# The last matrix of a decode step: w4 rows in four array columns, smaller last pieces, and a result stored in two parts

## The chip, the cores and the metric

The kernel runs on one core of a Trainium2 chip. A core has five engines that matter here: TensorE (PE in the profile; PEld is its loading of weights), VectorE (DVE), ScalarE (ACT), GpSimd (POOL) and SyncE (SP), which issues DMAs. Sixteen DMA engines move data between the chip's memory (HBM) and the core's on-chip memory (SBUF, 128 partitions). TensorE writes into eight accumulating banks (PSUM), from which VectorE and ScalarE read. The metric is the device time of one execution in microseconds, lower being better; three runs of the kernel before gave a median of 400.46 us.

## The reference

One token of a decode step, width D = 1024, all in bf16. The input is normalized, then goes through an attention block and an MLP-like block, and all are added:

```python
xn = _layernorm(x)
return x + A(xn) + B(xn)

# A: 32 query heads, 4 key/value heads, 65536 cached keys of 128
q = xn @ wq
o = softmax(q @ k.T * 128**-0.5) @ v
A = o @ wo                                  # wo: 4096 x 1024

# B: one token, so the shifts of the mixer leave zeros
h = gelu(layernorm(xn) @ w1)
x1 = xn + shifted(h) @ w2                   # shifted(h) is zero for one token
B = x1 + gelu(layernorm(x1) @ w3) @ w4      # w3: 1024 x 3584, w4: 3584 x 1024
```

So what is left after the attention is a row vector of 1024: the attention's result times wo, plus the activated row of 3584 times w4, plus two copies of normalized or plain x.

## The kernel before

Everything streams. SP issues all loads of the large arrays in one order (`stream`, line 285): wq, w3, w1 and w2, then eight pairs of K and V blocks of 8 MB each, then wo (8 MB) and w4 (7 MB). Three SBUF slots of 128 x 32768 bf16 take them in turn, so a load waits until the matmuls on what lay in its slot three loads earlier are done (`freed`, line 311). There is no scheduler: a small recorder (`Program`, line 49) takes each engine's instructions in the order in which the code names them, and `plan` (line 124) adds a semaphore wait only where a read or a write meets an earlier one of another engine or of a DMA.

For each K block, VectorE transposes it in 32x32 blocks and TensorE multiplies it with the queries into the bank tensor `sc` (four banks, `scores`, line 456); VectorE finds the maxima, ScalarE takes the exponentials, and TensorE multiplies with the V block into `oacc` (`values`, line 490). After a pair of blocks, `group_rows` (line 509) adds up a group of heads into `oT`, the attention's result laid out for a matmul.

What follows is the end of the kernel, and the place of the change. wo is 32 and w4 is 28 "rows": in row c, each partition holds 1024 numbers, and a column of 128 numbers (`oT[:, c]` or `hT[:, c]`) multiplies them. The stationary operand is that column repeated 32 times, so a matmul uses an array column of 32 out of 128 and leaves 32 equal rows in PSUM. `row_acc` (line 342) uses two array columns, j = 0 and 1, each for 512 of the 1024 result columns, and adds into the bank `psB`. Its first use is the w2 product (line 438), then wo (line 544), then the w4 rows up to the last `NARROW` = 8 (line 548).

The last eight w4 rows run in `narrow_rows` (line 554), in four array columns: q = 2h + j takes 256 result columns, h = 0 into the bank pm0 and h = 1 into pm1. After `AHEAD` = 5 of them, VectorE's sum of psB and the x part (`sums`, line 552) is added into pm0 and pm1 by two small matmuls with the selector `pick` (line 564), and the last three rows follow.

w4 comes in five loads, `W4_PIECES` = 8, 12, 5, 2 and 1 rows (line 299), all issued together as soon as the last K block is free. The pieces' matmuls wait for them one after the other. At the end ScalarE copies pm0's 256 columns to bf16 and VectorE pm1's, both into `x_halves` (lines 569 and 570), and ScalarE's queue issues one store of partitions 31 and 32, which hold the two halves of the result (line 571). Then ScalarE clears the semaphores and SP waits for the store to land (line 581).

Of the kernel before, what the change touches and what calls it, by code (L numbers as in the profile page):

```python
# [14 lines left out]
P = 128  # L15
ROW = 32768
SUBS = 4
SETS = 4
W4_PIECES = (8, 12, 5, 2, 1)
NARROW = 8  # L20
AHEAD = 5

WIDTH = {F32: 4, BF16: 2}

# [182 lines left out]
def kernel(  # L207
# [14 lines left out]
    nc = tc.nc  # L222
    D = A_x.shape[-1]
# [7 lines left out]
    FC = F // P  # L231
    UKEYS = P * ROW // DH
    assert DH == P and HQ // HKV == 8 and HKV == 4 and D == 1024 and F == 3584 and S == 1
    assert SK == 2 * UKEYS and sum(W4_PIECES) == FC
    NB = 2
# [3 lines left out]
    COLS = (P, 32)  # L239

    prog = Program(nc)
    pe, dve, act, pool = prog, prog.dve, prog.act, prog.pool

    def sb(name, shape, dtype=F32):
        return nc.alloc_sbuf_tensor(name, list(shape), dtype)

    def ps(name, shape):
        return nc.alloc_psum_tensor(name, list(shape), F32)
# [4 lines left out]
    x_row = sb("x_row", [32, D], BF16)  # L253
# [4 lines left out]
    x_halves = sb("x_halves", [64, 512], BF16)  # L258
    qdiag = sb("qdiag", [P, LEAD + 4 * P], BF16)
    g_col = sb("g_col", [P, 1], BF16)  # L260
# [9 lines left out]
    hT = sb("hT", [P, FC], BF16)  # L270
    oT = sb("oT", [P, 32], BF16)
    ol = sb("ol", [P, DH + 1])
    pick = sb("pick", [64, 2, 32])

    sc = ps("sc", [P, SUBS, 512])
    oacc = ps("oacc", [P, 512])
    pm = [ps(f"pm{i}", [P, 512]) for i in range(2)]
# [8 lines left out]
    tiles = {it: slots[i % 3] for i, it in enumerate(stream)}  # L286

    def load(it):
        t = tiles[it]
        if it == "wq":  # L290
            prog.load("sp", t[:], A_wq.rearrange("(p c) n -> p (c n)", c=DC))
        elif it == "w3":
            prog.load("sp", t[:, 0:DC * F], B_w3.rearrange("(p c) f -> p (c f)", c=DC))
        elif it == "w12":
            prog.load("sp", t[:, 0:DC * D], B_w1.rearrange("(p c) n -> p (c n)", c=DC))
            prog.load("sp", t[:, DC * D:2 * DC * D], B_w2.rearrange("(m c) n -> m (c n)", c=DC))
        elif it == "wo":
            prog.load("sp", t[:], A_wo.rearrange("(p j) n -> p (j n)", p=P))
        elif it == "w4":
            w4_v = B_w4.rearrange("(m c) n -> m c n", c=FC)  # L300
            c0 = 0
            for n in W4_PIECES:
                prog.load("sp", t[:, c0 * D:(c0 + n) * D], w4_v[:, c0:c0 + n, :].rearrange("p c n -> p (c n)"))
                c0 += n
        else:
            kind, i = it
            g, b = divmod(i, NB)
            cache = A_k_cache if kind == "K" else A_v_cache
            prog.load("sp", t[:], cache[0, g, b * UKEYS:(b + 1) * UKEYS, :].rearrange("(p ct) d -> p (ct d)", p=P))

    def freed(it):

        n = stream.index(it) + 3
        if n < len(stream):
            load(stream[n])

    load("wq")
    opening = len(prog.ops)

    dve.memset(x_row[:], 0.0)  # L320
    prog.load("act", x_row[0:1, :], A_x[0, 0:1, :])
    load("w3")
    load("w12")

# [9 lines left out]
    for b in range(2):  # L334
        pool.tensor_copy(
            out=spread[:, 2 * b:2 * b + 2, :].rearrange("p r (a i) -> p r a i", a=4),
            in_=ident_f[:, 64 * b:64 * b + 64].rearrange("p (i r) -> p r i", r=2).unsqueeze(2).to_broadcast([P, 2, 4, 32]))
    pool.memset(x_halves[:], 0.0)
    pool.memset(qdiag[:], 0.0)
    pool.memset(g_col[:], 0.0)  # L340

    def row_acc(j, lhsT, rhs, start=False):
        return pe.mm(psB[32 * j:32 * j + 32, :], lhsT.to_broadcast([P, 32]), rhs, start, False, (0, 32 * j), COLS)

    x_t = p_sb[:, 0:DC * 32].rearrange("p (c j) -> p c j", j=32)
    for a in range(4):
        dve.transpose(out=x_t[32 * a:32 * a + 32].rearrange("p c j -> p (c j)"),
                      in_=x_row[:, 256 * a:256 * (a + 1)].rearrange("p (i c) -> p c i", c=DC))
    dve.tensor_copy(out=xT[:], in_=x_t[:, :, 0])

    def layernorm(src, tag):
# [24 lines left out]
    _, xn2_rep, _, _ = layernorm(xn, "b")  # L376
# [6 lines left out]
                    in_=sel8[:].unsqueeze(1).unsqueeze(3).to_broadcast([P, 4, 8, 4]))  # L383
    dve.tensor_copy(out=pick[:],
                    in_=ident_f[0:64, 0:64].rearrange("p (j r) -> p j r", r=32)[:, :, 0:1].to_broadcast([64, 2, 32]))
    dve.tensor_scalar(out=ln_s1[:], in0=rstd1[:], scalar1=1.0, scalar2=None, op0=ALU.add)
    dve.tensor_tensor(out=ln_s2[:], in0=negmean1[:], in1=rstd1[:], op=ALU.mult)
    for j in range(2):
        dve.tensor_copy(out=x_halves[32 * j:32 * j + 1, :], in_=x_row[0:1, 512 * j:512 * (j + 1)])

    def row_matmul(rep, cols, widths):
        for c in range(DC):
# [37 lines left out]
    def compute_w12():  # L430
        wt = tiles["w12"][:, 0:2 * DC * D].rearrange("p (w c n) -> p w c n", w=2, c=DC)
        for c in range(DC):
            for q in range(2):
                pe.mm(sc[0:32, q, :], xn2_rep[:, c, :], wt[:, 0, c, 512 * q:512 * (q + 1)], c == 0, c == DC - 1,
                      (0, 0), COLS)
        h1 = p_sb[0:32, 0:1024].rearrange("p (q n) -> p q n", q=2)
        act.activation(out=h1, in_=sc[0:32, 0:2, :], func=ACTF.Gelu_apprx_tanh)
        for c in range(DC):
            for j in range(2):
                row_acc(j, g_col[:], wt[:, 1, c, 512 * j:512 * (j + 1)], start=(c == 0))  # L440
        freed("w12")

    W = ROW // SETS
# [80 lines left out]
    compute_wq()  # L524
    compute_w3()
    compute_w12()
    for u in range(NU):
        g, b = divmod(u, NB)
# [11 lines left out]
    o = tiles["w4"][0:64, FC * D:FC * D + D].bitcast(F32)  # L540
    dve.tensor_scalar(out=o, in0=x_halves[:], scalar1=ln_s1[0:64, 0:1], scalar2=ln_s2[0:64, 0:1],
                      op0=ALU.mult, op1=ALU.add)

    for j in range(32):
        for h in range(2):
            row_acc(h, oT[:, j:j + 1], tiles["wo"][:, D * j + 512 * h:D * j + 512 * (h + 1)])
    wt = tiles["w4"]
    for c in range(FC - NARROW):
        for j in range(2):
            row_acc(j, hT[:, c:c + 1], wt[:, D * c + 512 * j:D * c + 512 * (j + 1)])  # L550
    sums = og[0:64, :]
    dve.tensor_tensor(out=sums, in0=psB[0:64, :], in1=o, op=ALU.add)

    def narrow_rows(lo, hi, start=False):
        for c in range(lo, hi):
            for h in range(2):
                for j in range(2):
                    q = 2 * h + j
                    pe.mm(pm[h][32 * q:32 * q + 32, 0:256], hT[:, c:c + 1].to_broadcast([P, 32]),
                          wt[:, D * c + 512 * j + 256 * h:D * c + 512 * j + 256 * (h + 1)], start and c == lo, False,  # L560
                          (0, 32 * q), COLS)

    narrow_rows(FC - NARROW, FC - NARROW + AHEAD, start=True)
    for h in range(2):
        pe.mm32(pm[h][64 * h:64 * h + 64, 0:256], pick[:].rearrange("p j r -> p (j r)"),
                sums[:, 256 * h:256 * (h + 1)], False, False, (0, 64 * h))
    narrow_rows(FC - NARROW + AHEAD, FC)
    out_t = x_halves[:].rearrange("p (h n) -> p h n", h=2)
    act.copy(out=out_t[:, 0, :], in_=pm[0][0:64, 0:256])
    dve.tensor_copy(out=out_t[:, 1, :], in_=pm[1][64:128, 0:256])  # L570
    store = prog.store("act", out[0, 0, :].rearrange("(j n) -> j n", j=2), out_t[31:33].rearrange("p h n -> p (h n)"))

    prog.plan()
    with tc.tile_critical(sync_engine=mybir.EngineType.Pool, no_gpsimd_drain=True):
# [1 line left out]
    tc.close()  # L576
    tc.compile()
    prog.emit(opening, len(prog.ops))
    nums = sorted(s.num for s in prog.sems if s is not store.sem)
    nc.scalar.sem_clear(range(nums[0], nums[-1] + 1))  # L580
    nc.sync.add_instruction(mybir.InstEventSemaphore(
        name=nc.get_next_instruction_name(), engine=mybir.EngineType.SP, ins=[], outs=[],
        sync_info=mybir.SyncInfo(
            on_wait=[mybir.SyncWait(sync_type="semaphore", id=store.sem.num, ant_name=store.sem.name,
                                    wait_mode="sem-ge-imm", wait_value=16)],
            on_update=[mybir.SyncUpdate(sync_type="semaphore", id=store.sem.num, ant_name=store.sem.name,
                                        update_mode="sem-sub-imm", update_value=16)])))

# [1 line left out]
_INS = ['A_x', 'A_k_cache', 'A_v_cache', 'A_wq', 'A_wo', 'B_x', 'B_w1', 'B_w2', 'B_w3', 'B_w4']  # L590
# [26 lines left out]
```

## Time and profile before

| what | value |
|---|---|
| median of 3 runs | 400.46 us (400.43 to 400.66) |
| the profiled execution | 400.43 us, of which its span is 399.1 us |
| PE busy | 221.0 us (55%) |
| DVE busy | 210.2 us (53%) |
| ACT busy | 27.6 us (7%) |
| read from HBM | 169.87 MB, 426 GB/s over the span |
| loads on SP's queue (q1) | 98.7% of the sixteen DMA engines' span |
| mean granted TensorE clock | 0.798 |
| last w4 pieces, 1280, 512 and 256 KB | 33.5, 34.3 and 34.5 us from issue to landing |

The page of the profile gives busy times by engine, forty slices of the span, the DMA queues, the chain of work that ended last, and groups of instructions. The timeline shows single instructions with the idle time before them and what ended it, and the trace below it holds the time of each semaphore step and of each DMA packet. All times in them are microseconds from the start of the span unless ns is written.

### The profile page before, as it was taken

How to read it: one execution, taken by the hardware profiler on the slowest of the kernel's cores; microseconds unless marked ns; L12 is line 12 of the kernel's file. 1: busy time of each engine (PE TensorE's matmuls, PEld its weight loads, DVE VectorE, ACT ScalarE, POOL GpSimd, SP SyncE). 2: the span in 40 equal slices, each digit the busy share in tenths (PEclk: the TensorE clock that was granted, in tenths of full speed). 3: DMA queues.
4: the chain of work that ended last, by engine and by line, in shares of the span. 5: the costliest groups of instructions: out<-in, count | busy, mean ns of one | idle time of the engine just before them, and what ended most of it. 6: DMA issues, size and time to landing. Idle time of an engine off the chain costs nothing.

```text
span 399.1 us, 2559 instructions
## 1 busy us (share of the span) xinstructions
PE 221.0 (55%) x1360; PEld 45.5 (11%) x890; DVE 210.2 (53%) x156; ACT 27.6 (7%) x35; POOL 6.2 (2%) x29
## 2 busy tenths in 40 slices
PE   0250970592669246822874387429552946393586
PEld 0210010000201010011001100101010102010233
DVE  0520010975096549643963696359439932793411
ACT  1010030002000200020002000200010010002000
POOL 2000000000000000000000000000000000000000
PEclk9996895697659686968795679678966986597789
DMA  8989999999999999999999999999999999999996
GB/s 342 479 388 417 471 420 427 421 460 466 422 420 427 420 429 427 460 453 427 415 427 420 434 440 447 448 427 420 427 429 434 440 447 435 427 420 427 402 442 256
DMA packets 3760, 170.03 MB, mean 426 GB/s; under 512 B 419, under 2 KB 421, under 8 KB 678
## 3 DMA queue, kind: packets, MB, share of 16 engines
q1 hardware_dynamic: 3744, 169.87, 98.7%
q8 instruction: 9, 0.15, 0.1%
q14 instruction: 1, 0.01, 0.0%
q10 hardware_dynamic: 6, 0.00, 0.0%
HBM read 169.87 MB, written 0.00 MB: 426 GB/s over the span
## 4 chain that ended last, share of the span: by engine, by line
DMA 56%; DVE 21%; PE 17%; another core or an unknown queue 2%; ACT 2%; issue 0%; SPq 0%; POOLq 0%
DMA slot<-in_A_k_cache_dram 42%; DVE slot L82 15%; PE sc L106 12%; DMA slot<-in_B_w_dram 9%; DMA slot<-in_A_wq_dram 5%; PE oacc L106 4%; DVE p_sb L82 2%; DVE mx L82 2%; ACT p_sb L82 2%; PE pm L122 1%; DVE m L82 0%; DVE rep L82 0%; DVE nball L82 0%; DVE x_halves L82 0%
## 5 line engine op out<-in xcount | busy, mean ns | idle before, releaser
L82 DVE STREAM_TRANSPOSE slot<-slot 128x4096 f32<-128x4096 f32 x32 | 139.4, 4411 | 52.4 <-DMA slot<-in_A_k_cache_dram 52.3
L106 PE MATMUL sc<-slot,qdiag 128*128 128x512 bf16 x512 | 128.4, 410 | 69.7 <-DVE slot L82 69.6
L106 PE MATMUL oacc<-slot,p_sb 128*32 128x512 bf16 x512 | 44.9, 528 | 37.5 <-DVE negmg L82 18.8
L82 DVE STREAM_TRANSPOSE p_sb<-p_sb 128x2048 bf16<-128x2048 bf16 (+2 forms) x10 | 20.8, 2085 | 38.9 <-ACT p_sb L82 38.8
L82 DVE TENSOR_REDUCE mx<-sc 128x1 f32<-128x2048 f32 x8 | 18.3, 2292 | 29.7 <-PE sc L106 29.7
L102 PEld LDWEIGHTS <-qdiag 128*128 128x128 bf16 x128 | 13.0, 102 | 180.8 <-issue 180.8
L82 ACT ACTIVATE p_sb<-sc,nball 128x2048 bf16<-128x2048 f32 x8 | 15.7, 1967 | 250.7 <-DVE nball L82 250.7
L102 PEld LDWEIGHTS <-p_sb 128*32 128x32 bf16 x512 | 17.0, 128 | 62.1 <-issue 19.7
L106 PE MATMUL sc<-slot,ln_rep_b 128*32 128x512 bf16 (+1 forms) x80 | 16.2, 827 | 9.4 <-DMA slot<-in_B_w_dram 9.1
L82 DVE SCALAR_TENSOR_TENSOR og<-oacc,wb,og 128x512 f32<-128x512 f32 x4 | 3.0, 750 | 19.1 <-PE oacc L106 19.1
L122 PE MATMUL pm<-ident_f,mx 128*1 128x128 f32 x8 | 2.4, 296 | 19.1 <-DVE mx L82 19.1
L106 PE MATMUL psB<-slot,oT 128*32 128x512 bf16 x64 | 8.8, 443 | 1.3 <-DVE oT L82 1.3
L116 PE MATMUL pm<-ol,selx 128*128 128x129 f32 x8 | 2.3, 370 | 10.6 <-DVE ol L82 10.6
L82 DVE TENSOR_TENSOR og<-psB,slot 64x512 f32<-64x512 f32 x1 | 0.7, 683 | 13.8 <-PE psB L106 13.8
L106 PE MATMUL sc<-slot,ln_rep_a 128*32 128x512 bf16 x64 | 5.4, 512 | 4.5 <-DMA slot<-in_A_wq_dram 4.5
L116 PE MATMUL pm<-ln_rowsum_a,msk 128*128 128x1 f32 x2 | 0.6, 361 | 13.3 <-DVE ln_rowsum_a L82 13.3
L82 POOL COPY qdiag<-qx 32x32 bf16<-32x32 bf16 x16 | 3.2, 203 | 277.2 <-PE sc L106 251.1
L82 DVE STREAM_TRANSPOSE p_sb<-x_row 32x256 bf16<-32x256 bf16 x4 | 2.5, 616 | 7.4 <-DMA x_row<-in_A_x_dram 7.4
L106 PE MATMUL psB<-slot,hT 128*32 128x512 bf16 x40 | 4.7, 379 | 1.0 <-DMA slot<-in_B_w_dram 1.0
L122 PE MATMUL pm<-ident_f,rep 1*128 1x1 f32 x8 | 1.9, 240 | 5.0 <-DVE rep L82 5.0
L82 ACT COPY og<-oacc 128x512 f32<-128x512 f32 x4 | 2.3, 585 | 32.2 <-PE oacc L106 32.2
L102 PEld LDWEIGHTS <-ln_rep_b 128*32 128x32 bf16 x40 | 1.9, 112 | 22.9 <-issue 22.6
(86 smaller groups left out, 61.8 us busy)
## 6 DMA issues: line engine op xcount, KB each, us to landing
slot<-in_B_w_dram SPq DMA_DIRECT2D x1, 7168.0 KB, 37.4
slot<-in_B_w_dram SPq DMA_DIRECT2D x3, 2048.0 KB, 43.2
slot<-in_B_w_dram SPq DMA_DIRECT2D x1, 3072.0 KB, 33.8
slot<-in_B_w_dram SPq DMA_DIRECT2D x1, 1280.0 KB, 33.5
slot<-in_B_w_dram SPq DMA_DIRECT2D x1, 512.0 KB, 34.3
slot<-in_B_w_dram SPq DMA_DIRECT2D x1, 256.0 KB, 34.5
slot<-in_A_k_cache_dram SPq DMA_DIRECT2D x8, 42.1
slot<-in_A_v_cache_dram SPq DMA_DIRECT2D x8, 36.9
```

The costliest lines, as they stand in the source:

```text
L82: return program.add(Op(engine, lambda: method(*args, **kw), reads, writes, alone=kw.get("accum_out") is not None))
L102: self.add(Op("pe", lambda: pe.ldweights(lhsT, tile_position=pos), [lhsT], []))
L106: return pe.add_instruction(mybir.InstMatmult(name=nc.get_next_instruction_name(), engine=mybir.EngineType.PE, start_tensor_calc=start, st ...
L116: return self.add(Op("pe", lambda: pe.matmul(out, lhsT=lhsT, rhs=rhs, start=start, stop=stop, tile_position=pos, skip_group_check=True), [ ...
L122: return self.add(Op("pe", lambda: pe.transpose(out, in_, identity), [in_, identity], [out]))
```

## The change

The twenty w4 rows from the ninth on (`NARROW` = 20) now run in four array columns; twelve of them (`AHEAD` = 12) come ahead of the matmuls with `pick`. The halves of the result are cut in another way: array columns 0 and 1 hold result columns 0 to 511 (a = 0, 256 each), array columns 2 and 3 hold 512 to 1023 (a = 1). For that, `part` reads the two 256-column runs that belong to j out of a 1024-column row, in the w2, wo and early w4 products and in `x_halves`. The half a = 0 is in pm0 and is copied by VectorE. The half a = 1 is in two banks: 144 columns in pm1, copied by ScalarE, and 112 in sc, copied by VectorE. Each narrow row therefore takes six matmuls instead of four, with four loads of weights as before.

The loads of w4 are now 8, 12, 6, 1.5 and 0.5 rows; the last piece is the second half of the last row. The last two rows run for a = 0 first, then a = 1, and only the last row's a = 1 part reads the last piece. After a = 0 is copied, SP issues a store of it; after a = 1, ScalarE issues one. ScalarE waits for a new semaphore, `issued`, which SP raises behind its store, before it clears the semaphores; SP then waits for both stores.

```diff
@@ -16,9 +16,10 @@
 ROW = 32768
 SUBS = 4
 SETS = 4
-W4_PIECES = (8, 12, 5, 2, 1)
-NARROW = 8
-AHEAD = 5
+W4_PIECES = (8, 12, 6, 1.5, 0.5)
+NARROW = 20
+AHEAD = 12
+SHARE = 144
 
 WIDTH = {F32: 4, BF16: 2}
 
@@ -297,11 +298,12 @@
         elif it == "wo":
             prog.load("sp", t[:], A_wo.rearrange("(p j) n -> p (j n)", p=P))
         elif it == "w4":
-            w4_v = B_w4.rearrange("(m c) n -> m c n", c=FC)
-            c0 = 0
+            w4_v = B_w4.rearrange("(m c) n -> m (c n)", c=FC)
+            x0 = 0
             for n in W4_PIECES:
-                prog.load("sp", t[:, c0 * D:(c0 + n) * D], w4_v[:, c0:c0 + n, :].rearrange("p c n -> p (c n)"))
-                c0 += n
+                x1 = x0 + int(n * D)
+                prog.load("sp", t[:, x0:x1], w4_v[:, x0:x1])
+                x0 = x1
         else:
             kind, i = it
             g, b = divmod(i, NB)
@@ -338,6 +340,10 @@
     pool.memset(x_halves[:], 0.0)
     pool.memset(qdiag[:], 0.0)
     pool.memset(g_col[:], 0.0)
+
+    def part(rows, c, j):
+
+        return rows[:, D * c:D * (c + 1)].rearrange("p (a j n) -> p a j n", a=2, j=2)[:, :, j, :]
 
     def row_acc(j, lhsT, rhs, start=False):
         return pe.mm(psB[32 * j:32 * j + 32, :], lhsT.to_broadcast([P, 32]), rhs, start, False, (0, 32 * j), COLS)
@@ -386,7 +392,7 @@
     dve.tensor_scalar(out=ln_s1[:], in0=rstd1[:], scalar1=1.0, scalar2=None, op0=ALU.add)
     dve.tensor_tensor(out=ln_s2[:], in0=negmean1[:], in1=rstd1[:], op=ALU.mult)
     for j in range(2):
-        dve.tensor_copy(out=x_halves[32 * j:32 * j + 1, :], in_=x_row[0:1, 512 * j:512 * (j + 1)])
+        dve.tensor_copy(out=x_halves[32 * j:32 * j + 1, :].rearrange("o (a n) -> o a n", a=2), in_=part(x_row[0:1, :], 0, j))
 
     def row_matmul(rep, cols, widths):
         for c in range(DC):
@@ -437,7 +443,7 @@
         act.activation(out=h1, in_=sc[0:32, 0:2, :], func=ACTF.Gelu_apprx_tanh)
         for c in range(DC):
             for j in range(2):
-                row_acc(j, g_col[:], wt[:, 1, c, 512 * j:512 * (j + 1)], start=(c == 0))
+                row_acc(j, g_col[:], part(wt[:, 1, c, :], 0, j), start=(c == 0))
         freed("w12")
 
     W = ROW // SETS
@@ -541,34 +547,51 @@
     dve.tensor_scalar(out=o, in0=x_halves[:], scalar1=ln_s1[0:64, 0:1], scalar2=ln_s2[0:64, 0:1],
                       op0=ALU.mult, op1=ALU.add)
 
-    for j in range(32):
-        for h in range(2):
-            row_acc(h, oT[:, j:j + 1], tiles["wo"][:, D * j + 512 * h:D * j + 512 * (h + 1)])
+    for c in range(32):
+        for j in range(2):
+            row_acc(j, oT[:, c:c + 1], part(tiles["wo"], c, j))
     wt = tiles["w4"]
     for c in range(FC - NARROW):
         for j in range(2):
-            row_acc(j, hT[:, c:c + 1], wt[:, D * c + 512 * j:D * c + 512 * (j + 1)])
+            row_acc(j, hT[:, c:c + 1], part(wt, c, j))
     sums = og[0:64, :]
     dve.tensor_tensor(out=sums, in0=psB[0:64, :], in1=o, op=ALU.add)
 
-    def narrow_rows(lo, hi, start=False):
-        for c in range(lo, hi):
-            for h in range(2):
-                for j in range(2):
-                    q = 2 * h + j
-                    pe.mm(pm[h][32 * q:32 * q + 32, 0:256], hT[:, c:c + 1].to_broadcast([P, 32]),
-                          wt[:, D * c + 512 * j + 256 * h:D * c + 512 * j + 256 * (h + 1)], start and c == lo, False,
-                          (0, 32 * q), COLS)
-
-    narrow_rows(FC - NARROW, FC - NARROW + AHEAD, start=True)
-    for h in range(2):
-        pe.mm32(pm[h][64 * h:64 * h + 64, 0:256], pick[:].rearrange("p j r -> p (j r)"),
-                sums[:, 256 * h:256 * (h + 1)], False, False, (0, 64 * h))
-    narrow_rows(FC - NARROW + AHEAD, FC)
-    out_t = x_halves[:].rearrange("p (h n) -> p h n", h=2)
-    act.copy(out=out_t[:, 0, :], in_=pm[0][0:64, 0:256])
-    dve.tensor_copy(out=out_t[:, 1, :], in_=pm[1][64:128, 0:256])
-    store = prog.store("act", out[0, 0, :].rearrange("(j n) -> j n", j=2), out_t[31:33].rearrange("p h n -> p (h n)"))
+    parts = [[(pm[0], 0, 256, dve.tensor_copy)],
+             [(pm[1], 0, SHARE, act.copy), (sc[:, 0, :], SHARE, 256, dve.tensor_copy)]]
+
+    def narrow_row(c, a, start=False):
+        for bank, n0, n1, _ in parts[a]:
+            for j in range(2):
+                x0 = D * c + 512 * a + 256 * j
+                q = 2 * a + j
+                pe.mm(bank[32 * q:32 * q + 32, 0:n1 - n0], hT[:, c:c + 1].to_broadcast([P, 32]), wt[:, x0 + n0:x0 + n1],
+                      start, False, (0, 32 * q), COLS)
+
+    for c in range(FC - NARROW, FC - NARROW + AHEAD):
+        for a in range(2):
+            narrow_row(c, a, start=c == FC - NARROW)
+    for a in range(2):
+        for bank, n0, n1, _ in parts[a]:
+            pe.mm32(bank[64 * a:64 * a + 64, 0:n1 - n0], pick[:].rearrange("p j r -> p (j r)"),
+                    sums[:, 256 * a + n0:256 * a + n1], False, False, (0, 64 * a))
+    for c in range(FC - NARROW + AHEAD, FC - 2):
+        for a in range(2):
+            narrow_row(c, a)
+    out_t = x_halves[:].rearrange("p (a n) -> p a n", a=2)
+    stores = []
+
+    def finish(a, engine):
+        for bank, n0, n1, copy in parts[a]:
+            copy(out=out_t[:, a, n0:n1], in_=bank[64 * a:64 * a + 64, 0:n1 - n0])
+        stores.append(prog.store(engine, out[0, 0, 512 * a:512 * (a + 1)].rearrange("(j n) -> j n", j=2), out_t[31:33, a, :]))
+
+    narrow_row(FC - 2, 0)
+    narrow_row(FC - 1, 0)
+    finish(0, "sp")
+    narrow_row(FC - 2, 1)
+    narrow_row(FC - 1, 1)
+    finish(1, "act")
 
     prog.plan()
     with tc.tile_critical(sync_engine=mybir.EngineType.Pool, no_gpsimd_drain=True):
@@ -576,15 +599,26 @@
     tc.close()
     tc.compile()
     prog.emit(opening, len(prog.ops))
-    nums = sorted(s.num for s in prog.sems if s is not store.sem)
+    issued = nc.alloc_semaphore("issued")
+
+    def event(engine, kind, wait=None, update=None):
+
+        sem, value = wait or update
+        sync = dict(on_wait=[], on_update=[mybir.SyncUpdate(sync_type="semaphore", id=sem.num, ant_name=sem.name,
+                                                update_mode="sem-sub-imm" if wait else "sem-add-imm",
+                                                update_value=value)])
+        if wait:
+            sync["on_wait"] = [mybir.SyncWait(sync_type="semaphore", id=sem.num, ant_name=sem.name,
+                                              wait_mode="sem-ge-imm", wait_value=value)]
+        engine.add_instruction(mybir.InstEventSemaphore(
+            name=nc.get_next_instruction_name(), engine=kind, ins=[], outs=[], sync_info=mybir.SyncInfo(**sync)))
+
+    event(nc.sync, mybir.EngineType.SP, update=(issued, 1))
+    event(nc.scalar, mybir.EngineType.Activation, wait=(issued, 1))
+    nums = sorted(x.num for x in prog.sems if all(x is not y.sem for y in stores))
     nc.scalar.sem_clear(range(nums[0], nums[-1] + 1))
-    nc.sync.add_instruction(mybir.InstEventSemaphore(
-        name=nc.get_next_instruction_name(), engine=mybir.EngineType.SP, ins=[], outs=[],
-        sync_info=mybir.SyncInfo(
-            on_wait=[mybir.SyncWait(sync_type="semaphore", id=store.sem.num, ant_name=store.sem.name,
-                                    wait_mode="sem-ge-imm", wait_value=16)],
-            on_update=[mybir.SyncUpdate(sync_type="semaphore", id=store.sem.num, ant_name=store.sem.name,
-                                        update_mode="sem-sub-imm", update_value=16)])))
+    for y in stores:
+        event(nc.sync, mybir.EngineType.SP, wait=(y.sem, 16))
 
 # ---- launch: one core; inputs and outputs as the reference has them ----
 _INS = ['A_x', 'A_k_cache', 'A_v_cache', 'A_wq', 'A_wo', 'B_x', 'B_w1', 'B_w2', 'B_w3', 'B_w4']
```

## The prediction

> **What bounds the kernel now.** I read the page's slices and its chain of work first, then the chain in order of time near the end, then the timeline of the last seven microseconds, because the change touches only what follows the attention part.
>
> ```profile
> DMA  8989999999999999999999999999999999999996
> DMA 56%; DVE 21%; PE 17%; another core or an unknown queue 2%; ACT 2%; issue 0%; SPq 0%; POOLq 0%
> ```
>
> The loads are busy in every slice but the last: 170 MB at 426 GB/s is the span. What a change in the tail can win is only what stands behind the last load. The end of the chain of work:
>
> ```profile
> 362.59 34.50 DMA slot<-in_B_w_dram
> 397.08 0.04 issue
> 397.13 0.34 PE pm L106 x4
> 397.47 0.02 issue
> 397.49 0.43 DVE x_halves L82
> ```
>
> The last piece of w4 lands at 397.08, four matmuls follow, then a copy, then the store. The timeline gives the rest:
>
> ```profile
> 392.15 2.77 PE L106 MATMUL psB<-slot,hT 128*32 128x512 bf16 x24 [1.02 <-DMA slot<-in_B_w_dram]
> ...
> 394.96 0.68 DVE L82 TENSOR_TENSOR og<-psB,slot 64x512 f32<-64x512 f32 x1 [13.81 <-PE psB L106]
> 395.25 0.73 PE L106 MATMUL pm<-slot,hT 128*32 128x256 bf16 x20 [0.34 <-DMA slot<-in_B_w_dram]
> ...
> 396.50 0.40 PE L106 MATMUL pm<-slot,hT 128*32 128x256 bf16 x8
> 397.13 0.29 PE L106 MATMUL pm<-slot,hT 128*32 128x256 bf16 x4 [0.23 <-DMA slot<-in_B_w_dram]
> ...
> 397.45 0.36 ACT L82 CAST x_halves<-pm 64x256 bf16<-64x256 f32 x1 [26.45 <-PE pm L106]
> 397.49 0.43 DVE L82 CAST x_halves<-pm 64x256 bf16<-64x256 f32 x1 [1.85 <-PE pm L106]
> 397.95 0.26 ACTq L93 DMA_DIRECT2D out_dram<-x_halves  x1
> ```
>
> TensorE waits for a piece each time and is done before the next lands. From the last landing (397.084) to the last record (SP's wait for the store, 399.097 to 399.114) are 2.03 us: 0.043 to the first matmul, 0.293 for the four, 0.072 to VectorE, its 0.426, 0.032 to the issue, 1.147 from the issue to SP's wait passing, 0.017. Nothing else in the kernel can move the end, unless the last landing moves. The execution took 400.43 us, so 1.33 lie outside the span of 399.1; the median of the runs is 0.03 higher.
>
> **The last landing.** The pieces become 8, 12, 6, 1.5 and 0.5 rows instead of 8, 12, 5, 2 and 1: the same bytes, five transfers, eight packets of each per DMA engine. The trace's packets of 24, 16, 10, 4 and 2 KB took 912, 611, 387, 159 and 84 ns: 37.5 ns per KB and 9 ns each. By that line 12, 3 and 1 KB take 459, 121 and 47 ns, 627 together, against 630 now: no change. Bounds for the 1 KB packet: 47 by the line, 54 by the store's 1 KB packet, 84 if it took as long as one of 2 KB; eight of them add 0 to 0.3 us. I take 0, the line, since all five sizes lie on it. So the last piece lands at 397.08, and the one ahead of it 8 x 43 ns (packets start 4 ns before the one ahead ends) earlier, at about 396.73.
>
> **Rows 8 to 19** move from 24 matmuls of 512 columns in two array columns (0.2155 us per row) to 72 of 256, 144 and 112 in four. Five such rows of 20 matmuls started 0.108 us apart, so twelve take 1.3 us instead of 2.6, from 392.13 on. If the split into 144 and 112 cost two further issues at 0.036 each (0.73 us over 20), a row takes 0.18 and twelve take 2.2. Both end before the six-row piece lands (about 395.8): nothing on the path. VectorE's sum moves from 394.96 to about 391.2, behind the eighth row, and the matmuls with pick (now three, 0.65 us for two) to 393.5; neither was on the path. Six rows then take 0.65 to 1.1 us, to 396.45 or 396.9; only the far end would touch the next piece, by 0.2 us.
>
> **The tail.** Matmuls on the 1.5-row piece start at 396.77. Rows 26 and 27 of the first half come first, 0.118 apart, and the second lasts 0.272: pm0 is done at 397.165. VectorE starts 0.072 later (as now) and copies 64x256 in 0.426: 397.24 to 397.66. Row 26 of the other half is finished by about 397.2. The half-row piece lands at 397.08; matmuls start at 397.127, two of 144 columns and, 0.06 later, two of 112. A matmul lasts its columns at 2.4 GHz plus 0.165 (256: 0.272; 512: 0.379), so they end at 397.36 and 397.405. ScalarE starts at 397.40; its rows of 64x256 (0.365) and 128x512 (0.585) give 0.27 for 144: done at 397.67. VectorE's 112 columns (0.426 less 144 x 1.05 ns, from 158 ns for one column and 426 for 256) take 0.275, and could start at 397.48, **but VectorE is still at the other half until 397.66**: this is the new wait. It copies from 397.68 to 397.95 (0.013 between two copies, as the two x_halves copies at 20.4 stand), where it ended at 397.92. So the shorter copy, 0.15 us less, is given back by the queue on VectorE: +0.03. Bounds: -0.17 if the first copy were done before 397.48; +0.2 if the six rows come late as above.
>
> **The stores.** SP issues the first at 397.70, and it lands by 398.85 at ACT's 1.15 us: slack 0.27. ACT issues the second at 397.98 (two packets of 512 B for two of 1 KB, 54 ns each: about -0.02). Its wait for SP's "issued" passes at once, and only the clearing of semaphores (0.17 us, over by 398.5) stands behind it. SP's second wait costs 0.017, within what is there. Bounds: 0, or +0.24 if the two stores' way from issue to packets (0.48 us on ACT) is passed one after the other. I take -0.02, as the queues differ. x_halves' halves laid out anew, and psB's columns read in two runs of 256, cost nothing: same counts, far from the end.
>
> Sum: 0 + 0 + 0.03 - 0.02 = +0.01 on 400.43: 400.44, and 400.47 beside the median.
>
> **Rival 1, slower: the ninth instruction packet.**
>
> ```profile
> q8 instruction: 9, 0.15, 0.1%
> ```
>
> The sixteen landings of each load spread over 0.6 us at 39 us of the span. After each 16 KB instruction packet one more DMA engine lands 1.5 us late, each time another one; after one 8 KB packet, one lands 0.95 late. At the end eight engines are 1.7 to 2.0 us behind the first, one 1.2, seven at most 0.54, and the late ones set 397.08. The ninth packet starts at 396.46, when TensorE passes into its last 24 matmuls, and hits nothing. TensorE's list grows from 1744 to 1846 instructions, so that point now falls in rows 8 to 19, at about 393.0, with loads under way. On a seventh early engine it costs nothing (0.54 + 1.5 is about 2.0); on the half-late one +0.7 (401.15); on a late one +1.5 us: **401.97**. Eight of eight fell on different engines, which speaks for an early one. Chances 0.09 late, 0.04 half-late. [...]
>
> **Rival 2: the clock halves in the tail.**
>
> ```profile
> 374.63:378.04 3.41, 1.62 (x32) 0.55 (x24) 1.66 (x3) 0.00 (x0) 0.00 (x0) 1.00 0.86 370
> 391.69:395.11 3.42, 2.77 (x24) 1.34 (x24) 0.15 (x1) 0.00 (x0) 0.00 (x0) 1.00 0.95 390
> 395.11:398.52 3.41, 1.94 (x36) 0.96 (x35) 0.96 (x2) 0.36 (x1) 0.00 (x0) 1.00 0.23 88
> ```
>
> These are stretches between moments at which the granted clock can change (columns: length, then busy time of PE, PEld, DVE, ACT and POOL, clock, DMA share, GB/s). After the third the clock fell to 0.50, after the first two not. Without the 0.165 us that each burst's last matmul adds, the third holds some 1.3 us of streaming and the first 1.45. The changed middle stretch would hold 1.8, so it should stay; with the stretches lying 1.7 us later, one would hold some 1.2 and the clock would fall near 396.8. At half clock a row takes 0.213 and a matmul 0.1 longer: +0.1 to +0.3 there, and +0.58 (401.05) if the six rows ran so too. Chance 0.10. [...]
>
> **Rival 3: the stores queue on each other**, +0.24: 400.7. Chance 0.05.
>
> **How the numbers follow.** Forecast 0.69 (400.25 to 400.8 by its bounds), rival 1 0.13, rival 2 0.10, rival 3 0.05, and 0.03 for a gain over 0.8 us, of which I see no mechanism: it would need the late engines early. A measurement of this kernel tells about 0.2%, 0.8 us, from no change. Slower by more than that is the late engine alone, 0.09; faster 0.03; within 0.88. The range runs from 400.2 to 401.0: the forecast with its bounds, rival 3 and most of rival 2.
>
> **What would show it.** In the changed profile: the last landing of w4 at 397.1; twelve narrow rows in 1.3 us from 392.1; VectorE's two last copies back to back, the second ending near 397.95 and well after its matmuls; ScalarE's before it; ACT's issue at about 398.0, SP's some 0.3 earlier. Wrong would be: a last landing at 397.8 or 398.6 with the ninth instruction packet near 393 (rival 1), a clock of 0.50 ahead of 397.4 (rival 2), or VectorE's second copy ending before 397.8 (a gain up to 0.2).

## The result, and the profile after

The changed kernel is slower: 401.81 us median of 6 runs (401.66 to 402.17) against 400.46 (400.31 to 400.66); the ratio is 1.0034, 95% interval 1.0024 to 1.0045. The forecast was 400.47 with a range of 400.2 to 401.0; the time lies near the first rival's 401.97. The profiled execution took 401.68 us.

The page of the changed kernel: the span, the DMA slices and the queue of instruction packets.

```profile
span 400.4 us, 2656 instructions
...
DMA  8989999999999999999999999999999999999895
...
q8 instruction: 9, 0.15, 0.1%
```

As many instruction packets as before, 9 of them, and the same bytes from HBM, 169.87 MB. The chain of work of the changed kernel near its end (start, length, what):

```profile
362.61 35.93 DMA slot<-in_B_w_dram
398.54 0.04 issue
398.58 0.24 PE pm L107 x2
398.82 0.06 PE sc L107 x2
398.88 0.02 issue
398.91 0.28 DVE x_halves L83
```

The last piece lands at 398.54 instead of 397.08: +1.46. What follows it takes 1.83 us instead of 2.03: -0.20. The sum, +1.26, is the whole difference of the spans (400.37 and 399.11). The timeline of the changed kernel shows which landing is late:

```profile
396.84 0.29 PE L107 MATMUL pm<-slot,hT 128*32 128x256 bf16 x4 [0.18 <-DMA slot<-in_B_w_dram]
...
397.27 0.42 DVE L83 CAST x_halves<-pm 64x256 bf16<-64x256 f32 x1 [4.06 <-PE pm L107]
397.72 0.32 SPq L94 DMA_DIRECT2D out_dram<-x_halves  x1
398.58 0.24 PE L107 MATMUL pm<-slot,hT 128*32 128x144 bf16 x2 [1.35 <-DMA slot<-in_B_w_dram]
398.58 0.09 PEld L103 LDWEIGHTS <-hT 128*32 128x32 bf16 x1 [1.56 <-issue]
398.64 0.23 PE L107 MATMUL sc<-slot,hT 128*32 128x112 bf16 x2
398.86 0.28 ACT L83 CAST x_halves<-pm 64x144 bf16<-64x144 f32 x1 [27.94 <-PE sc L107]
398.91 0.28 DVE L83 CAST x_halves<-sc 64x112 bf16<-64x112 f32 x1 [1.22 <-PE sc L107]
399.22 0.26 ACTq L94 DMA_DIRECT2D out_dram<-x_halves  x1
```

Up to the 1.5-row piece (matmuls from 396.84) all is as forecast. Then TensorE waits 1.35 us for the half-row piece, 128 KB. Each load raises its semaphore sixteen times in the trace, read here as once for each of the sixteen DMA engines' shares, and the matmuls wait for the last of these landings: here 398.54, and they start at 398.58. The sixteen landings of that last load, in us behind the first, from the trace's semaphore records:

```
before   0 .16 .19 .20 .27 .37 .54 | 1.19 | 1.70 1.74 1.86 1.90 1.91 1.95 1.99 2.00
changed  0 .01 .04 .08 .11 .17 .34 | 1.18 | 1.54 1.55 1.57 1.62 1.64 1.69 1.76 3.27
```

Seven early, one half-late, eight late in both; in the changed kernel one of the late ones is later by another 1.5. The packets show what stands there. By the times in these traces, most packets start 3 or 4 ns before another one ends (13 to 16 ns where that one is an instruction packet). Where that other one is taken as the packet ahead on the same DMA engine, neighbours can be told (start, ns, bytes; q8 is the instruction queue):

```
changed   396.225   46   1024      first of eight of the last piece
          396.268 1086  16384 q8
          397.340  138   1024
          397.463  111   1024      ... five more, 105 to 135 ns
          398.088    9      4      semaphore
before    396.451    9      4      semaphore, last of its engine
          396.457 1095  16384 q8
```

By that reading, the ninth packet in the kernel before began just as a late engine had finished all its data. In the changed one it began seven packets too early, and those seven took 105 to 138 ns each instead of 46.

### The profile page after: what moved, and what is told of

Its sections match the earlier page's. It is cut to its first block, busy times and chain, and to the rows that moved or that the text cites. A ratio compares the mean times of both kernels' runs of the same rounds, so it can differ in the third digit from the quotient of the medians.

```text
span 400.4 us, 2656 instructions
## 1 busy us (share of the span) xinstructions
PE 221.8 (55%) x1426; PEld 46.3 (12%) x916; DVE 210.5 (53%) x157; ACT 27.5 (7%) x35; POOL 6.2 (2%) x29
## 3 DMA queue, kind: packets, MB, share of 16 engines
q1 hardware_dynamic: 3748, 169.87, 98.4%
HBM read 169.87 MB, written 0.00 MB: 424 GB/s over the span
## 4 chain that ended last, share of the span: by engine, by line
DMA 57%; DVE 24%; PE 14%; another core or an unknown queue 2%; ACT 2%; issue 0%; SPq 0%; POOLq 0%
DMA slot<-in_A_k_cache_dram 42%; DVE slot L83 19%; PE sc L107 9%; DMA slot<-in_B_w_dram 9%; DMA slot<-in_A_wq_dram 5%; PE oacc L107 4%; DVE p_sb L83 2%; DVE mx L83 2%; ACT p_sb L83 2%; PE pm L123 1%; DVE m L83 0%; DVE rep L83 0%; DVE nball L83 0%; DVE x_halves L83 0%
## 5 line engine op out<-in xcount | busy, mean ns | idle before, releaser
L107 PE MATMUL oacc<-slot,p_sb 128*32 128x512 bf16 x512 | 46.0, 539 | 37.5 <-DVE p_sb L83 18.8
L107 PE MATMUL pm<-slot,hT 128*32 128x144 bf16 (+1 forms) x80 | 3.1, 250 | 3.0 <-DMA slot<-in_B_w_dram 3.0
```

The source lines that it names most:

```text
L107: return pe.add_instruction(mybir.InstMatmult(name=nc.get_next_instruction_name(), engine=mybir.EngineType.PE, start_tensor_calc=start, st ...
```

## The experiments

Three theories: the **instruction packet** (TensorE's list is 92 records longer, so the ninth packet is asked for earlier and runs ahead of data on an engine already late); the **pieces** (small last packets); the **new tail** (split copies, two stores). All experiments are compared with the kernel before on the same chip (medians 400.50 to 400.53).

**The list alone.** In the kernel before, behind the w2 product:

```diff
+    for i in range(92):
+        spot = (0, 32 * (i % 4))
+        prog.add(Op("pe", lambda spot=spot: nc.tensor.ldweights(g_col[:].to_broadcast([P, 32]), tile_position=spot), [g_col[:]], []))
+    prog.held.clear()
     for u in range(NU):
```

> The kernel before with 92 more loads of weights in TensorE's list, put behind the w2 product, where TensorE idles for some 14 us; nothing else changes. Theory (instruction packet): TensorE's list is now as long as the changed kernel's (it has 92 records more than before in the trace), so the ninth 16 KB packet is asked for some 92 instructions earlier, while the w4 loads are still running, is served on the DMA engine that the first packet had already made late, and the last landing moves from 397.1 to about 398.5: +1.2 to +1.6 us. Rival (pieces): no change, 400.4 to 400.6. Rival (new tail: split copies, two stores, the wait on SP): no change either.

Measured: 402.46 (401.72 to 403.05, 4 runs), ratio 1.0048, 1.0032 to 1.0064. Its chain of work (the execution of 401.72):

```profile
362.69 35.70 DMA slot<-in_B_w_dram
398.38 0.04 issue
398.43 0.34 PE pm L106 x4
398.77 0.02 issue
398.79 0.43 DVE x_halves L82
```

The landing moves to 398.38 with the old pieces, copies and store. The ninth packet runs at 392.19, and from the five-row piece on one of the sixteen landings, 1.85 behind the first up to the twelve-row piece, is 3.34 behind. This refutes both rivals as the main cause. Two of the four runs took 403.0; why those had 1.3 us more isn't known, as only the execution of 401.72 has a profile.

**The pieces alone.** The kernel before with the w4 loads of the changed one:

```diff
-W4_PIECES = (8, 12, 5, 2, 1)
+W4_PIECES = (8, 12, 6, 1.5, 0.5)
```

> The kernel before with only the w4 pieces changed to 8, 12, 6, 1.5 and 0.5 rows; the same instructions on TensorE. Theory (instruction packet): the ninth packet is asked for in the third of the last eight rows, at about 396.0, behind the last data packets of its engine: no late landing, within 0.15 us of before. Rival (pieces): the half-row piece of 1 KB packets is what lands late, +1.2 to +1.5 us. Rival (new tail): no change.

Measured: 400.75 (eight of 10 runs 400.69 to 400.85, two 401.88 and 401.89), ratio 1.0011, 1.0002 to 1.0021. Not 1.3 us, but 0.25 in most runs where 0.15 at most was expected. Its chain shows what:

```profile
395.99 0.04 issue
396.04 0.73 PE pm L106 x20
396.76 0.58 PE pm L116 x4
397.35 0.50 PE pm L106 x12
397.84 0.02 issue
397.86 0.42 DVE x_halves L82
```

The six-row piece lands at 395.99 and TensorE is busy from then to the end: the matmuls with pick (L116) stand behind it. Narrow rows that put pick ahead of that piece, twelve in the changed kernel, are needed for its pieces; one or two, below, are nearly enough. The two runs of 401.9 have spans of 399.2 and 399.5 us, as short as the others', so what they have more lies outside the span and isn't a late landing.

**The old pieces in the changed kernel.** `W4_PIECES = (8, 12, 5, 2, 1)`, all else as changed.

> The changed kernel with the w4 pieces of before (8, 12, 5, 2, 1 rows). Theory (instruction packet): TensorE's list is as long as in the changed kernel, the ninth packet is asked for near 392.9 and served near 396.2 with some packets of 2 KB left behind it: +1.0 to +1.6 us over before. Rival (pieces): back to before, within 0.2 us. Rival (new tail): still +1.3.

Measured: 402.09 (400.74 to 402.45, 10 runs), ratio 1.003, 1.002 to 1.0041. Four runs took 400.74 to 401.14, six 402.08 to 402.45. The profiled one is of the first sort (400.95): its ninth packet began at 396.61, and the last landing was at 397.27, 2.11 behind the first. The two levels would fit a race: the packet falls ahead of the data or behind it. The slower one has no profile, so that its landing is late is inferred. Even the faster one is 0.2 to 0.6 above before: the last row lands as a whole, and VectorE's two copies, at 397.63 and 398.08, follow it.

**Fewer narrow rows.** `NARROW = 8`, `AHEAD = 5`, all else as changed.

> The changed kernel with 8 narrow rows instead of 20 (5 of them ahead of the sum), everything else as changed: pieces, split banks and copies, two stores. Theory (instruction packet): rows 8 to 19 take 48 instructions again instead of 120, so the ninth packet is asked for near 396.0 and falls behind the data: the last landing is at 397.1 and the time is before's within 0.15 us. Rival (pieces): still +1.2 to +1.5 us. Rival (new tail): still +1.2 to +1.5 us.

Measured: 400.98 (400.81 to 401.21), ratio 1.0012, 1.0003 to 1.0022. No late landing (397.18; the packet at 396.98, behind the data). But 0.5 above before, not 0.15: pick stands behind the six-row piece again (its matmuls from 396.64), and VectorE's two copies follow each other, from 397.77 to 398.50.

**The forecast's tail without the packet.** `NARROW = 9`, `AHEAD = 1`, all else as changed, so TensorE's list is shorter.

> The changed kernel with 9 narrow rows (1 ahead of the sum), split banks, split copies, pieces and stores as changed: the recorded forecast's tail without the packet in its way. Theory: last landing at 397.1 to 397.2, VectorE's two copies back to back, 400.4 to 400.65 (forecast's tail +0.01, and up to 0.1 more because the matmuls with pick end near 396.1, after the six-row piece has landed). Rival (the split copies and two stores cost by themselves): above 401.

Measured: 400.69 (400.44 to 401.1, 11 runs), ratio 1.0005, 0.9996 to 1.0013. The timeline:

```profile
397.31 0.42 DVE L83 CAST x_halves<-pm 64x256 bf16<-64x256 f32 x1 [1.78 <-PE pm L107]
397.48 0.28 ACT L83 CAST x_halves<-pm 64x144 bf16<-64x144 f32 x1 [26.27 <-PE sc L107]
397.76 0.32 SPq L94 DMA_DIRECT2D out_dram<-x_halves  x1
397.76 0.28 DVE L83 CAST x_halves<-sc 64x112 bf16<-64x112 f32 x1
398.07 0.26 ACTq L94 DMA_DIRECT2D out_dram<-x_halves  x1
```

Here is the wait that the forecast named: VectorE's 112 columns start when its 256 are done, 0.3 after ScalarE starts. The stores, issued 0.31 apart, landed 0.30 apart (SP's waits passed at 398.90 and 399.20), so they don't queue on each other. Last landing 397.16.

**ScalarE alone on the second half**, with 10 narrow rows:

```diff
-    parts = [[(pm[0], 0, 256, dve.tensor_copy)],
-             [(pm[1], 0, SHARE, act.copy), (sc[:, 0, :], SHARE, 256, dve.tensor_copy)]]
+    parts = [[(pm[0], 0, 256, dve.tensor_copy)],
+             [(pm[1], 0, 256, act.copy)]]
```

> The changed kernel with 10 narrow rows (2 of them ahead of the sum) and the half a = 1 in one bank of 256 columns, copied by ScalarE alone; pieces and two stores as changed. TensorE's list then has 64 instructions between row 8 and the six-row piece, where the changed kernel has 132 and the kernel before 48. Theory (instruction packet): it is asked for so late that it runs behind the data; the last landing is at 397.1 to 397.2. VectorE's first copy no longer stands ahead of the second half: ScalarE copies from 397.45 to 397.82 and the store is issued near 397.85, 0.1 earlier than before: 400.25 to 400.45. If the number of narrow rows or TensorE's list does not matter: +1.2 to +1.5 us.

Measured: 400.59 (400.29 to 401.68, 11 runs), ratio 1.0003, 0.9995 to 1.0012; the highest is the profiled one, whose packet ran at 400.99, behind the span of 399.2. From the last landing (397.22) to the store's issue (397.99) are 0.76 us, before 0.87: the 0.1 is there, but the landing itself lies anywhere from 397.08 to 397.28 in the profiles without a late one, whatever the pieces, and hides it.

**The same with the old pieces:**

> As the run with 10 narrow rows and ScalarE alone on the second half, but with the pieces of before (8, 12, 5, 2, 1 rows). Theory: the last row lands as a whole, so both halves of the last row and row 26's second half wait for it: TensorE ends near 397.5, ScalarE's copy near 397.9, 400.4 to 400.6; the smaller pieces alone are worth some 0.1 us. If the packet of instructions is hit by the shorter data queue: +1.0 to +1.5 in some runs.

Measured: 400.71 (400.5 to 400.81), ratio 1.0003, 0.9994 to 1.0012. The difference to the smaller pieces is 0.12 us, as expected, but no more than the noise, so a gain from them isn't shown.

**Forty loads of weights** instead of 92 in the kernel before:

> The kernel before with 40 more loads of weights behind the w2 product, in TensorE's idle time. Theory (instruction packet): it is asked for 40 instructions earlier, near 394.0 instead of 395.5, and starts some 1 to 3 us after that, at or before the end of its engine's data at 396.4: late landings of 0.5 to 1.5 us in at least some of the runs, so times on two levels, 400.4 to 400.7 and 401.0 to 402.0. If the packet does not matter: all within 0.2 us of before.

Measured: 401.86 (400.63, then 401.52 to 402.06, 6 runs), ratio 1.0033, 1.0021 to 1.0045: two levels. The profiled run is the 400.63; its packet began at 396.37 and delayed nothing. In the five others, which have no profile, forty instructions without any work for the result cost about as much as the whole change.

**Ten packets:** 340 loads of weights.

> The kernel before with 340 more loads of weights behind the w2 product, in TensorE's idle time; TensorE's list then needs ten 16 KB packets ahead of the end of the data, the ninth near 365 and the tenth near 392. Theory (the packets go round eight engines): the ninth and tenth fall on the engines that the first and the second made late, so in the landings of the last load two engines of sixteen are some 3.0 to 3.7 us behind the first, six or seven 1.5 to 2.1, and the number of early engines stays seven; time +1.2 to +2.6 us. Rival (they go round all sixteen, as the recorded forecast took it): two more engines are 1.5 to 2.1 late, five stay early, none is over 2.3, time within 0.2 us of before.

Measured: 401.81 (401.69 to 401.88), ratio 1.0033, 1.0021 to 1.0045. The page's line of instruction packets:

```profile
q8 instruction: 10, 0.16, 0.2%
```

The landing of the last piece is at 398.48. The ninth packet, at 374.48, is read as one on an engine already late again: in the landings of wo, which come next, one is 3.43 behind the first and seven are early as before, so this packet made no fresh engine late. The tenth ran only at 396.34 and made no second engine that late, so the expectation of two failed. Three traces of three with a ninth packet ahead of the end of its data have such a landing: 3.27 behind the first in the changed kernel, 3.34 with 92 loads of weights, 3.43 here. The records don't name engines, but the overlaps of 3 or 4 ns, read as above, can be followed backwards. From the ninth packet they lead through the first in the changed kernel (43.48) and in the kernel before (43.36), and from the tenth here through the second (63.24). With 92 loads of weights, the engine that went from 1.85 to 3.34 is by its lateness that of the first packet, 1.83 to 1.86 behind in all loads since the one after that packet. Only the ninth here can't be told: the engines of the first and the fourth packet lie within 0.03 us.

**A shorter list.** ScalarE alone as above, 18 narrow rows (10 ahead), and at the start:

```diff
-        for c in range(DC):
-            for q in range(2):
-                pe.mm(sc[0:32, q, :], xn2_rep[:, c, :], ...)
-        h1 = ...
-        act.activation(out=h1, in_=sc[0:32, 0:2, :], func=ACTF.Gelu_apprx_tanh)
-        for c in range(DC):
+        for c in range(1):
             for j in range(2):
```

> The changed kernel with 18 narrow rows (10 ahead of the sum), the second half in one bank copied by ScalarE alone, and 39 instructions less at the start: it leaves out the w1 product with its gelu (one token, the shifts leave zeros, nothing reads it) and the w2 product's matmuls for c = 1 to 7 (their stationary operand is zero). With 18 rows in four array columns the theory still finds the ninth packet asked for only when the six-row piece has landed, so it runs behind the data: 400.25 to 400.5, up to 0.2 below before. If four array columns for many rows, or the pieces, cost by themselves: above 401.2.

Measured: 400.56 (400.26 to 400.8, 11 runs), ratio 1.0000, 0.9991 to 1.0009.

```profile
q8 instruction: 8, 0.13, 0.1%
```

The page's line of instruction packets: within the span only eight are left, and the last landing is 1.92 behind the first. Eighteen rows in four array columns and small pieces cost nothing that can be measured without the packet. No version here beat the kernel before by what can be measured, and the medians of this run, of 9 narrow rows and of the two with 10 lie 0.04 to 0.14 above what was expected.

## Why the prediction was wrong

**The step that failed** stands in rival 1: "Eight of eight fell on different engines, which speaks for an early one." By the landings, the ninth fell on a late one, in the changed kernel (some 1.8 plus 1.5: 3.27) as with 92 and 340 loads of weights (3.34 and 3.43). Eight different engines had been taken for the start of a round of sixteen; the traces fit a round of eight, the ninth packet on the engine of the first and the tenth on that of the second; why eight, no run shows. The number that would have followed was worked out, 401.97 for a late engine, but got a chance of 0.09. The kernel before bore a hint: its ninth packet began 6 ns after a semaphore packet, the last of a late engine, and so by the overlaps was on a late engine itself; the forecast only noted that it "hits nothing".

**"that point now falls in rows 8 to 19, at about 393.0".** Steps of 256 matmuls and loads of weights from packet to packet are the author's estimate; in the kernel before, the eight packets behind the first ran 211 to 344 of TensorE's records apart, 259 in the mean. Counted in such steps from the first packet's place, TensorE passed that point at 392.92, but the packet ran at 396.27. In the kernel before, too, it had passed the point at 395.49, not at the packet's 396.46. (By the records the list grows from 2250 to 2342, by 92 and not by 102.) In all twelve traces the later packets ran 0.4 to 5.9 us after TensorE had passed their point as estimated, but for two that ran over 9 us after it; what they wait for is not settled. By the author's estimate such a delay can make the outcome a race when the point lies some 1 to 4 us ahead of the end (the two levels with 40 loads of weights and with the old pieces).

**"No change" of the landing by smaller packets: right.** Packets of 12, 3 and 1 KB took 465, 121 and 46 ns in the median (459, 121 and 47 by the line).

**Rows 8 to 19: right.** Their matmuls started from 392.12 to 393.52, 0.11 us a row; the split cost at most 0.004 a row.

**The tail: right in its mechanism, untested by the change itself.** There the half row came so late that VectorE was free, and the tail was 0.20 shorter. In the changed kernel matmuls of 144 and 112 columns took 0.226 and 0.213 us in the median, 0.225 and 0.212 by the forecast's line (0.272 and 0.379 for 256 and 512: 0.418 ns a column). Without the packet the two copies follow each other (0.42 and 0.28 us), 0.03 apart instead of 0.013. The forecast's +0.01 stands against +0.16 measured with 9 narrow rows, where pick is a part of it, with an interval that holds both.

**Rival 2, the clock: did not come.** The changed kernel's stretches (PE busy is the second number, the clock stands ahead of the DMA share):

```profile
392.82:396.23 3.41, 1.99 (x78) 1.61 (x52) 0.39 (x1) 0.00 (x0) 0.00 (x0) 1.00 0.78 315
396.23:399.64 3.41, 1.11 (x36) 0.49 (x15) 0.69 (x2) 0.28 (x1) 0.00 (x0) 1.00 0.07 17
```

After the first the clock stayed, though the row is but 0.05 us busier than the one after which it fell before; it fell after the second, with all matmuls done. Between its first and its last change in the two traces, every stretch of one clock lasts a whole multiple of 3.41 us, up to 17.07. At the clock of 0.50 the wo rows of the kernel before started 0.43 us apart (381.55 to 384.53), at 1.00 0.215, and a matmul of 512 columns took 0.634 us, at 1.00 0.379; the forecast's 0.213 for a row and 0.1 for a matmul of 256 columns are estimates in line with these.

**Rival 3, stores that queue: refuted**. With 9 narrow rows they are 0.31 apart at the issue and 0.30 at the end; with ScalarE alone and small pieces, 0.17 (397.82 and 397.99) and 0.18 (398.96 and 399.14).

## What to carry to other kernels

Where loads fill the span, count the instructions too. Here TensorE's 2250 records in the kernel before came with nine 16 KB instruction packets, 2590 with ten; such a packet took 0.9 to 1.1 us in the kernels before and after, and one that ran ahead of data of its engine, as read here, left one of the sixteen landings some 1.5 us later. The matmuls wait for the last of the sixteen. Before adding instructions anywhere ahead of the end of the loads (the 40 and 92 stood behind the w2 product, near the start), look where the last instruction packet lies against the end of its engine's data. A gain of 0.1 us behind the last landing was not seen here, where the landing itself varied by 0.2 (397.08 to 397.28).

## What the runs showed of the hardware

The sixteen landings of a load lie on three levels. Of the last load's in the kernel before, seven lie within 0.54 us, one is 1.19 behind the first and eight 1.70 to 2.00. The single one came with the 8 KB instruction packet at 75.32: no landing lay between 0.56 and 1.87 behind the first in the load that lands from 68.25, one at 1.23 in the next, from 87.60. In the loads behind each of the first eight 16 KB packets one more landing is late, by some 1.5 us. The 16 KB packets took 0.92 to 1.10 us in the kernels before and after; in the kernel before, the 64 KB packets behind six of them, by the overlaps, took 2.9 to 3.0 us instead of 2.4. The lateness was not made up there while the loads ran on: the first landing and the last were 1.86 to 2.08 us apart in every load from 44 us of the span to its end. In the changed kernel one such packet cost 1.5 us on the path of the data.
